# The triangular solves of chunks 2, 4, 6 and 8 handed to the scheduler six operations a step instead of four

## The chip, the cores and the metric

The program runs on one core of a Trainium2 chip. The metric is the device time of one execution in microseconds. The core's engines have instruction queues of their own, which they work off in order: PE (the TensorE, matmuls), DVE (the VectorE), ACT (the ScalarE), POOL (GpSimd) and SP. Here POOL and SP mostly issue DMA transfers.

## The reference

A delta-rule attention over 768 positions (4 batches, 8 heads, 48 features), then two feed-forward blocks on the 3072 resulting rows:

```python
for t in range(S):
    kt, vt, bt = k_n[:, :, t], v[:, :, t], beta[:, :, t, None]
    y[:, :, t] = np.einsum('bhd,bhde->bhe', q[:, :, t], state)
    v_old = np.einsum('bhde,bhd->bhe', state, kt)
    state = state + bt[..., None] * np.einsum('bhd,bhe->bhde', kt, vt - v_old)
# x: y as 3072 rows of 384
h = np.maximum(x @ w_in, 0.0);  x = (h * h) @ w_out          # 384 -> 2048 -> 384
h = np.maximum(np.maximum(x @ w1, x @ w2), x @ w3);  out = h @ w_out2   # 384 -> 768 -> 384
```

## The kernel before

The 768 positions are cut into 12 chunks of 64. Within a chunk the recurrence becomes a triangular system, and its inverse is what the **solve** finds: `solve32` takes two chunks at once (its blocks are 32 x 32), loads the products of keys from DRAM into a tile in `buf`, scales them (`prep`, from ss in L257 to L248), and eliminates column by column (`solve`): 30 steps of one multiply (L278) and one add (L280) on the DVE, then a last multiply (L281). `finish32` stores the result to the DRAM tensor xt (L318, four DMAs on SP's queue). For `HALVED[g]`, that is chunks 2g and 2g + 1, the solve runs in chunk 2g - 2 of the main loop: the solve in chunk 4 is for chunks 6 and 7.

`attention(c)` does the rest of chunk c in ten pieces. `load_x` loads xt into the tile xb (L335, four DMAs on POOL's queue). `st0` multiplies the loaded v by the norms (L421, on the DVE), then does the matmuls pA and pY (L432) and the subtraction r = v - pA (L435, DVE). `zz` makes the transpose xT of xb (L391, DVE) and the matmuls pZ (L398), `ww` the matmuls pW; `mm_u` and `st2` make the outputs and the new state Sb (L467, DVE), and `st3` transposes them and splits them into xh and xl (L507, DVE), the inputs of the feed-forward block. v and kq have two buffers each, and the load of a v (L353, POOL) waits until r has read the one before it in the same buffer.

`moe_a(c)` is the first feed-forward block for chunk c. For each of eight `fp` there is a group `s1` of 18 matmuls into p (L537), then three ACT operations of which the last writes gh (L543), then gl = p - gh on the DVE (L544); two groups later, `s2` makes 18 matmuls of gh and gl into px (L555). p has two buffers, so a group of p waits for the gl of the group before the last. At the chunk's end px is copied to xs and stored (L569, L570).

In the main loop (L773) chunk c runs `moe_a(c)` as the main line with 16 steps, and `steps` (L573) deals the others out beside it: at each step, each of the others has a rate added to its account and is advanced once for every whole number in it. attention(c + 1) has the rate 9/15. A solve in chunk 2, 4, 6 or 8 had the rate 4. Ten advances go by after its loads (`landing=10`), then one for `prep` and one for each step of the elimination. This sets the order in which the operations are written; a scheduler that works with a simulated timeline then sets where each stands in its engine's queue. From chunk 9 on, `load_w3s` loads the weights of the second block (raw, L89, on SP's queue) into a pool of three buffers, which xs shares. After chunk 11 the second block runs (L830, L847).

Of the kernel before, what the change touches and what calls it, by code (L numbers as in the profile page):

```python
# [38 lines left out]
def delta_moe(ctx, tc, kc, ab, kt, vt, beta, beta32, beta16, kq, w_in, w_out, w1, w2, w3, w_out2, out):  # L39
# [157 lines left out]
    def kkps(cs, ps_, dma=nc.sync):  # L197

        todo = [(c, p) for c in cs for p in range(2)]
        ahead = len(kcts) - (len(kcts) < 4)  # L200
        for n in range(min(ahead, len(todo))):
            kkp_load(*todo[n], dma)
        for n, (c, p) in enumerate(todo):
            ks = kss[nk[1] % len(kss)]
            nk[1] += 1
            pk, pq = kk_matmul(c, p, ps_[n % len(ps_)])
            kk_ends[0] = act.copy(ks[:, 0], pk).ins
            kk_ends[1] = vec.tensor_mul(out=ks[:, 1], in0=pq, in1=mask.unsqueeze(1).broadcast_to([128, U2, C])).ins
            for i in mul_after:
                behind(kk_ends[1], i)  # L210
            yield
            kk_store(c, p, ks[:, 0], dma)

            for t in range(2):
                dma.dma_start(p_d[c][64 * t:64 * t + 64, U2 * p:U2 * p + U2], ks[64 - 64 * t:128 - 64 * t, 1])
            if n + ahead < len(todo):
                kkp_load(*todo[n + ahead], dma)
            yield
# [354 lines left out]
    def steps(main, *others):  # L573

        due = [0.0] * len(others)
        for _ in main:
            for i, (rate, g) in enumerate(others):
                due[i] += rate
                while due[i] >= 1.0:
                    due[i] -= 1.0  # L580
                    next(g, None)
        for _, g in others:
            for _ in g:
                pass
# [7 lines left out]
    def w3load(ws):  # L592
        todo = []

        def turned():
            if after:
                after[:], abs_after[:] = last_gl, last_gh
            raw, i, fs = todo.pop(0)
            turn(raw, wh[i][:, :, fs], wl[i][:, :, fs], (KD, 128), vec)

        for i in ws:
            w = (late if i < 2 else wb).tile([128, 2, KD, F2], F32R, name=f"w3_{i}", tag="ABC"[i])
            wh[i], wl[i] = w[:, 0], w[:, 1]
            for f in range(NF2):
                fs = slice(128 * f, 128 * (f + 1))
                todo.append((fetch(w3s[i][:, :, 256 * f:256 * (f + 1)], (KD, 128), nc.sync), i, fs))
                if len(todo) > 1:
                    turned()
                yield
        turned()  # L610

    def load_x2(n, pool_):
        x_h = pool_.tile([128, KD, BT], F32R, name="x_h", tag="x_h")
        x_l = pool_.tile([128, KD, BT], F32R, name="x_l", tag="x_l")
        for j in range(2):
            js = slice(j * TB, (j + 1) * TB)
            xr = conv.tile([128, KD, TB], F32, name="xr", tag="raw", bufs=NR)
            nc.sync.dma_start(xr, x2_d[2 * n + j])
            act.copy(x_h[:, :, js], xr)
            vec.tensor_sub(out=x_l[:, :, js], in0=xr, in1=x_h[:, :, js].bitcast(F32))  # L620
        return x_h, x_l

    def part(g, n):
        for _ in range(n):
            next(g, None)
            yield

    def drain(g):
        for _ in g:
            pass  # L630

    if True:
# [18 lines left out]
        def solve32(g, load=(nc.sync, nc.sync), store=((nc.sync,) * 2,) * 2, landing=0):  # L651
            M, a, ready, norm = start32(g, load)
            for _ in range(landing):
                yield
            if landing:
                prep_after[:] = last_gl
            nm = ready()
            if not landing:
                normed.append(norm(nm))
            yield  # L660
            for n, i in enumerate(solve(vec, M, 32, 64 * len(HALVED[g]), a, tmp32)):
                for j in solve_after:
                    behind(i.ins, j)
                ops.append(i.ins)
                if landing and n == 12:
                    norm(nm)
                yield
            finish32(g, M, store)

        def later(n, g):  # L670
            for _ in range(n):
                yield
            yield from g
# [3 lines left out]
        def weights():  # L677
            for f in range(NF):
                if last_gl[0] and last_gl[0] not in gls:
                    gls.append(last_gl[0])  # L680
                after[:] = gls[-2:-1]
                words(1)
                load_wout(f, vec, nc.sync)
                after.clear()
                prep_after[:] = solve_after[:] = parted[-1:]
                yield
# [86 lines left out]
        for c in range(NC):  # L773
            extra = []
            if c + 1 < NC:
                extra.append((9 / 15.0, attention(c + 1)) if c > 1 else (13 / 15.0, later(3, attention(1))) if not c else (17 / 15.0, later(8, attention(2))))
            if c == 0:
                ws = weights()
                for _ in range(2):
                    next(ws)  # L780
                extra.insert(0, (1.0, ws))
            if c in KK:
                extra.append((1.0, kkps(HALVED[1], (at,), pool)) if c == 0 else (0.8, later(5, kkps(HALVED[2], (at,)))) if c == 1 else (0.6, kkps(HALVED[KK[c]], (at,))))
            if c in SOLVE:
                solve_next = solve32(SOLVE[c], landing=10) if c else solve32(1, (pool,) * 2)
                extra.append((5.0, later(45, part(solve_next, 20))) if c == 0 else (4.0, solve_next))
            if c == 1:
                extra.insert(0, (6.0, solve_next))
            if c == 1:
                kc_after.clear()  # L790
            if c == 1:
                solve_after[:] = last_vec
                prep_after.clear()
            if c == 2:
                solve_after.clear()
            if c == 9:
                after[:] = last_gl
                load_w3s = w3load((0, 1))
            if 9 <= c < NC - 1:
                extra.append((0.4, part(load_w3s, 6)))  # L800
            if c == NC - 1:
                pr.close()
                wb = ctx.enter_context(tc.tile_pool(name="wb", bufs=1, side="right", reuse_waits="tile"))
                drain(load_w3s)
                after.clear()
                abs_after.clear()
                extra.append((0.5, w3load((2,))))
                first = load_x2(0, wb)
            steps(moe_a(c, gp), *extra)
# [112 lines left out]
```

## Time and profile before

| | us |
|---|---|
| median of 3 runs (1000.75 to 1005.13) | 1004.14 |
| the profiled execution | 1003.58 |
| its span, from the first to the last instruction | 1001.9 |
| PE busy | 917.8 |
| DVE busy | 461.1 |
| ACT busy | 407.3 |
| POOL busy | 129.9 |

The first number is what a change is measured by; the sums are made on the profiled execution. Busy time of an engine is time in which at least one of its instructions ran; that of the PE includes waits inside its pipeline. An idle time on the list of an engine's instructions stands in square brackets behind the instruction that ended it, with what that instruction waited for.

### The profile page before, as it was taken

Reading aid. Unit: us, or ns where it says so; the run is one execution under the profiler, and the core shown is the slowest. Engines: PE = TensorE matmul, PEld = TensorE weight load, DVE = VectorE, ACT = ScalarE, POOL = GpSimd, SP = SyncE. Lnnn points to the kernel's source line nnn. Section 1 sums busy time; section 2 is a strip of 40 time slices with the busy share of each in tenths; the row PEclk is TensorE's granted clock in tenths of the full one; section 3 lists DMA queues with packets and bytes.
Section 4 is the critical chain, followed back from the end, with each engine's and each line's share of the span. In section 5 each row is a group of like instructions: output and inputs, shape, how many; then the busy total and the mean of one; then the engine's idle time right before and its main releaser. Section 6 shows DMA issues by size and latency. Waiting matters only on the chain.

```text
span 1001.9 us, 26561 instructions
## 1 busy us (share of the span) xinstructions
PE 917.8 (92%) x11674; PEld 844.7 (84%) x11674; DVE 461.1 (46%) x992; ACT 407.3 (41%) x789; POOL 129.9 (13%) x213
## 2 busy tenths in 40 slices
PE   4067889999999999999999799979999999999998
PEld 4057778999899989999999799979888888888887
DVE  2979796138324832483249144462732323232221
ACT  1947643444444444444453355553521212121111
POOL 2222311121121112112211120000200000000000
PEclk8568988999999999999999899999999999999999
DMA  8938722651463246315621532142400100000001
GB/s 186 329 88 252 226 82 58 163 141 53 133 172 93 60 126 168 97 54 140 152 73 65 122 109 84 49 142 64 152 16 16 47 16 32 17 14 19 9 25 40
DMA packets 74916, 97.25 MB, mean 97 GB/s; under 512 B 35520, under 2 KB 53232, under 8 KB 74800
## 3 DMA queue, kind: packets, MB, share of 16 engines
q1 hardware_dynamic: 54688, 54.22, 19.5%
q0 software_dynamic: 11584, 34.90, 12.3%
q10 hardware_dynamic: 8528, 6.42, 2.2%
q8 instruction: 92, 1.51, 0.6%
q14 instruction: 24, 0.20, 0.1%
HBM read 70.88 MB, written 24.64 MB: 95 GB/s over the span
## 4 chain that ended last, share of the span: by engine, by line
PE 59%; issue 5%; DMA 4%; DVE 3%; POOL 1%; ACT 1%; POOLq 0%; DVEq 0%; ACTq 0%; SPq 0%
PE p L830 23%; PE px L555 12%; PE p L537 12%; PE po L847 8%; DMA xb<-xt 1%; PE pU L442 1%; PE pW L411 1%; PE pY L482 1%; PE pZ L398 1%; DMA v<-in_vt_dram 1%; DVE buf L280 1%; DVE buf L278 1%; DMA xt<-buf 1%; PE pk L190 1%; DVE gl L544 0%
## 5 line engine op out<-in xcount | busy, mean ns | idle before, releaser
L555 PE MATMUL px<-gh,wout 128*128 128x256 f32 x1152 | 219.1, 289 | 4.3 <-ACT gh L543 4.3
L830 PE MATMUL p<-x_h,w 128*128 128x512 f32 x648 | 203.5, 395 | 0.0
L555 PEld LDWEIGHTS px<-gh,wout 128*128 128x128 f32 x1152 | 179.8, 192 | 7.5 <-ACT gh L543 4.7
L537 PE MATMUL p<-xh,win_h 128*128 128x256 f32 x576 | 172.0, 299 | 7.1 <-DVE gl L544 4.9
L537 PE MATMUL p<-xl,win_h 128*128 128x256 f32 x576 | 167.8, 294 | 4.8 <-DVE xl L507 4.8
L537 PE MATMUL p<-xh,win_l 128*128 128x256 f32 x576 | 167.3, 291 | 0.0
L555 PE MATMUL px<-gl,wout 128*128 128x256 f32 x576 | 163.2, 283 | 0.0
L830 PEld LDWEIGHTS p<-x_h,w 128*128 128x128 f32 x648 | 121.6, 188 | 27.2
L544 DVE TENSOR_TENSOR gl<-p,gh 128x512 fp32r<-128x512 f32 x96 | 65.7, 686 | 153.8 <-ACT gh L543 153.8
L830 PE MATMUL p<-x_l,w 128*128 128x512 f32 x324 | 128.1, 395 | 0.0
L537 PEld LDWEIGHTS p<-xh,win_h 128*128 128x128 f32 x576 | 115.1, 200 | 10.8 <-DVE gl L544 6.0
L541 ACT ACTIVATE p<-p 128x512 f32<-128x512 f32 x96 | 55.8, 582 | 158.6 <-PE p L537 157.6
L537 PEld LDWEIGHTS p<-xl,win_h 128*128 128x128 f32 x576 | 114.5, 200 | 6.1 <-DVE xl L507 4.9
L537 PEld LDWEIGHTS p<-xh,win_l 128*128 128x128 f32 x576 | 115.3, 200 | 0.1
L555 PEld LDWEIGHTS px<-gl,wout 128*128 128x128 f32 x576 | 110.7, 192 | 0.0
L836 DVE TENSOR_TENSOR mx<-p,mx 128x512 f32<-128x512 f32 x36 | 24.9, 691 | 128.1 <-PE p L830 127.9
L838 ACT CAST hh<-mx 128x512 fp32r<-128x512 f32 x36 | 22.3, 620 | 126.4 <-DVE mx L837 126.4
L830 PEld LDWEIGHTS p<-x_l,w 128*128 128x128 f32 x324 | 61.0, 188 | 14.5
L278 DVE TENSOR_TENSOR buf<-buf 128x30 f32<-128x30 f32 (+9 forms) x180 | 59.4, 330 | 5.5
L280 DVE TENSOR_TENSOR buf<-buf 128x30 f32<-128x30 f32 (+9 forms) x180 | 59.5, 330 | 5.2
L543 ACT CAST gh<-p 128x512 fp32r<-128x512 f32 x96 | 56.3, 586 | 2.7
L542 ACT ACTIVATE p<-p 128x512 f32<-128x512 f32 x96 | 55.9, 583 | 2.8
(153 smaller groups left out, 1331.9 us busy)
## 6 DMA issues: line engine op xcount, KB each, us to landing
kq<-in_kc_dram POOLq DMA_DIRECT2D x22, 448.0 KB, 4.3
raw<-in_moe_w_dram SPq DMA_DIRECT2D x18, 384.0 KB, 3.3
p<-p POOLq DMA_DIRECT2D x22, 256.0 KB, 3.2
raw<-in_moe_w_out_dram SPq DMA_DIRECT2D x14, 384.0 KB, 3.6
v<-in_vt_dram POOLq DMA_DIRECT2D x24, 192.0 KB, 4.4
ktp<-in_kt_dram POOLq DMA_DIRECT2D x24, 192.0 KB, 3.3
xr<-x SPq DMA_DIRECT2D x12, 384.0 KB, 3.1
out_dram<-os ACTq DMA_DIRECT2D x24, 192.0 KB, 1.9
```

What stands on the lines that cost most here:

```text
L278: eng.tensor_tensor(out=tv, in0=M[:, 0:j, j].unsqueeze(2).broadcast_to([u, j, m]), in1=M[:, j, j + 1:n].unsqueeze(1).broadcast_to([u, j, m ...
L280: yield eng.tensor_tensor(out=M[:, 0:j, j + 1:n], in0=M[:, 0:j, j + 1:n], in1=tv, op=ALU.add)
L537: pe.matmul(p1[:, j], w[:, k, f], x[c][:, k], start=n == 0 and j == 0, stop=n == 8, skip_group_check=True)
L541: act.activation(out=p1, in_=p1, func=AF.Relu)
L542: act.activation(out=p1, in_=p1, func=AF.Square)
L543: last_gh[0] = act.copy(gh, p1).ins
L544: last_gl[0] = vec.tensor_sub(out=gl, in0=p1, in1=gh.bitcast(F32)).ins
L555: pe.matmul(acc[m], w, x[:, j], start=f == 0 and i == 0 and m != 1, stop=f == NF - 1 and i == 2, skip_group_check=True)
L830: pe.matmul(p, w[i][:, k, fs], x[:, k], start=n == 0, stop=n == 8)
L836: vec.tensor_max(out=t, in0=ps[1], in1=t)
L838: act.copy(hh[:, f], t2)
L847: pe.matmul(po[:, 0:DM], x[:, f, js], w[:, f], start=i == 0, stop=i == 17)
```

## The change

One number in L786: the rate of the solves in chunks 2, 4, 6 and 8. The solve of chunk 0, which goes on in chunk 1, has its own rates.

```diff
             if c in SOLVE:
                 solve_next = solve32(SOLVE[c], landing=10) if c else solve32(1, (pool,) * 2)
-                extra.append((5.0, later(45, part(solve_next, 20))) if c == 0 else (4.0, solve_next))
+                extra.append((5.0, later(45, part(solve_next, 20))) if c == 0 else (6.0, solve_next))
```

The same instructions are made; some stand elsewhere in the queues of PE, DVE, ACT and SP. POOL's order is the same.

On the DVE at the start of the solve in chunk 4 (gl is the first block's, ss and r are the solve's; - is before, + is the change):

```order
 L544 TENSOR_TENSOR gl<-p_4227,gh 128x512
 L544 TENSOR_TENSOR gl<-p_4260,gh 128x512
-L544 TENSOR_TENSOR gl<-p_4338,gh 128x512
 L257 COPY ss<-buf 128x32
```

The solve's first operation now stands ahead of one gl more; chunks 2, 6 and 8 have the same piece.

On the DVE at the end of the same solve, where chunk 5 begins (Sb and xl end the attention of chunk 5, xT and r belong to that of chunk 6, v to that of chunk 7, both gl to chunk 5):

```order
 L281 TENSOR_TENSOR buf<-buf,a_4252 128x1024
-L507 TENSOR_TENSOR xl<-pT,xh 128x3x128
-L435 TENSOR_TENSOR r<-v,pA 128x384
-L391 STREAM_TRANSPOSE xT<-xb 128x512
+L467 TENSOR_TENSOR Sb<-pD,Sb 128x384
+L507 TENSOR_TENSOR xl<-pT,xh 128x3x128
+L391 STREAM_TRANSPOSE xT<-xb 128x512
+L435 TENSOR_TENSOR r<-v,pA 128x384
+L421 TENSOR_TENSOR v<-v,normT 128x384
 L544 TENSOR_TENSOR gl<-p_4971,gh 128x512
 L544 TENSOR_TENSOR gl<-p_4996,gh 128x512
-L421 TENSOR_TENSOR v<-v,normT 128x384
```

xT now stands ahead of r, and v, which stood behind the two gl, ahead of them. Chunk 7 begins in the same way. In chunk 3 v stood between the two gl before, and the last gl of chunk 2 now stands behind L281; in chunk 9 v now stands between the first gl and the second.

On the PE at the start of chunk 9 (p_8106 is its second group of p, p_8184 its third, pZ the attention's):

```order
 L537 MATMUL p_8106<-xl,win_h 128x256
-L555 MATMUL px<-gh,wout_791 128x256 x2
-L398 MATMUL pZ<-xb,k_8133 32x32
+L398 MATMUL pZ<-xb,k_8133 32x32 x21
+L555 MATMUL px<-gh,wout_791 128x256 x2
+L398 MATMUL pZ<-xb,k_8133 32x32 x11
 L537 MATMUL p_8184<-xh,win_h 128x256
```

All the pZ now stand ahead of the third group; before, the rest of them stood behind it.

On SP's queue at the same place (xt is the solve's result, raw a load of weights, x the store of xs):

```order
 L318 DMA xt_128<-buf 32x1024 x2
+L89 DMA raw<-in_moe_w_dram 128x3x256 x2
 L570 DMA x_137<-xs 128x512
 L570 DMA x_137<-xs 128x256
-L89 DMA raw<-in_moe_w_dram 128x3x256 x7
+L89 DMA raw<-in_moe_w_dram 128x3x256 x5
```

Two of the loads of weights now stand ahead of the store of xs.

## Rows read from the trace of the kernel before

**Rows 1.** The page, busy us (share of the span) and instructions of two engines.

```profile
PE 917.8 (92%) x11674; PEld 844.7 (84%) x11674; DVE 461.1 (46%) x992; ACT 407.3 (41%) x789; POOL 129.9 (13%) x213
```

**Rows 2.** Timeline of PE: start, us, what, [idle before and its releaser].

```profile
262.92 0.39 PE L537 MATMUL p<-xh,win_h 128*128 128x256 f32 x1 [1.26 <-DVE gl L544]
269.00 0.39 PE L537 MATMUL p<-xh,win_h 128*128 128x256 f32 x1 [0.38 <-DVE gl L544]
362.50 0.38 PE L537 MATMUL p<-xh,win_h 128*128 128x256 f32 x1 [2.16 <-DVE gl L544]
461.23 0.39 PE L537 MATMUL p<-xh,win_h 128*128 128x256 f32 x1 [0.21 <-DVE gl L544]
563.48 0.28 PE L398 MATMUL pZ<-xb,k 32*32 32x32 f32 x2 [5.90 <-DMA xb<-xt]
```

**Rows 3.** Windows: us, busy of each engine, PEclk (granted), DMA share, GB/s.

```profile
core 0: us, PE busy (x) PEld busy (x) DVE busy (x) ACT busy (x) POOL busy (x), PEclk, DMA share, GB/s
360.00:365.00 5.00, 2.84 (x39) 2.70 (x32) 2.63 (x5) 1.55 (x3) 0.29 (x1) 0.86 0.92 260
365.00:370.00 5.00, 5.00 (x90) 4.83 (x89) 1.11 (x2) 2.02 (x4) 0.00 (x0) 0.80 0.33 82
```

**Rows 4.** The chain of waits in order of time: start, us, what.

```profile
357.24 3.82 DMA xb<-xt
...
457.51 2.35 DMA xb<-xt
...
555.69 7.02 DMA xb<-xt
...
571.44 2.34 PE p L537 x18
```

**Rows 5.** Timeline of DVE, end of the solves in chunks 2 and 4.

```profile
253.58 1.22 DVE L281 TENSOR_TENSOR buf<-buf,a 128x1024 f32<-128x1024 f32 x1
...
334.22 0.69 DVE L544 TENSOR_TENSOR gl<-p,gh 128x512 fp32r<-128x512 f32 x1 [0.75 <-ACT gh L543]
...
338.22 0.41 DVE L280 TENSOR_TENSOR buf<-buf 128x240 f32<-128x240 f32 x1
338.66 0.41 DVE L278 TENSOR_TENSOR buf<-buf 128x240 f32<-128x240 f32 x1
...
351.03 0.55 DVE L467 TENSOR_TENSOR Sb<-pD,Sb 128x384 f32<-128x384 f32 x1
...
352.77 1.23 DVE L281 TENSOR_TENSOR buf<-buf,a 128x1024 f32<-128x1024 f32 x1
...
355.18 0.55 DVE L435 TENSOR_TENSOR r<-v,pA 128x384 f32<-128x384 f32 x1 [0.53 <-PE pA L432]
361.16 0.71 DVE L391 STREAM_TRANSPOSE xT<-xb 128x512 f32<-128x512 f32 x1 [5.42 <-DMA xb<-xt]
```

**Rows 6.** Timelines of POOL, DVE and SP: loads issued, and v waiting for its load.

```profile
258.58 2.61 POOL L335 DMA_DIRECT2D xb<-xt  x4 [7.63 <-DMA xt<-buf]
261.18 0.55 POOL L351 DMA_DIRECT2D kq<-in_kc_dram  x1
261.72 0.58 POOL L353 DMA_DIRECT2D v<-in_vt_dram  x1
...
267.79 0.56 DVE L421 TENSOR_TENSOR v<-v,normT 128x384 f32<-128x384 f32 x1 [4.93 <-DMA v<-in_vt_dram]
...
356.57 2.62 POOL L335 DMA_DIRECT2D xb<-xt  x4 [6.93 <-DMA xt<-buf]
...
392.29 0.54 POOL L351 DMA_DIRECT2D kq<-in_kc_dram  x1 [5.47 <-PE pY L432]
394.19 0.55 POOL L353 DMA_DIRECT2D v<-in_vt_dram  x1 [1.36 <-DVE r L435]
397.20 0.56 DVE L421 TENSOR_TENSOR v<-v,normT 128x384 f32<-128x384 f32 x1 [2.84 <-DMA v<-in_vt_dram]
...
555.12 2.65 SPq L89 DMA_DIRECT2D raw<-in_moe_w_dram  x3
```

## The prediction, made before the changed kernel was run

> **What bounds the kernel now.** I read the page's busy times first: the TensorE (PE) is busy for 92% of the span, the VectorE (DVE) for 46% [rows 1]. So a change on the DVE pays only where the PE stands still for it. The PE's own list of instructions comes next, for the idle time ahead of each [rows 2]. It stands still at the four places where a chunk with a solve has ended and the next has begun: 1.26 us at the start of chunk 3 (and 0.38 us at 269.00), 2.16 us in chunk 5, 0.21 us in chunk 7 and 5.90 us in chunk 9. I call these places A, B, C and D. After B and D the PE also runs slowly: the granted clock is 0.86 and 0.80 in the two stretches after B's stall [rows 3], so it had fallen to the 1.2 GHz level and come back to 2.4. At B that costs 5 x 0.14 + 5 x 0.20 = 1.7 us.
>
> The chain of waits and the DVE's own list tell what happens there. The solve's last multiply (L281) starts at 352.77 [rows 5]; its result is stored to DRAM, loaded again as xb, and the transpose xT, which stands in the DVE's queue ahead of the next chunk's gl, starts at 361.16 after 5.42 us of idling [rows 5]. Eight microseconds pass between solve and transpose. The PE waits for that gl because p has two buffers and gl frees one. At D the load alone takes 7.02 us, at B 3.82, at C 2.35 [rows 4]: three w3 loads (raw) are issued beside it at D [rows 6].
>
> **The change, part by part.** Nothing is added or removed; the solve is only handed over earlier. In the order on the DVE, ss (the solve's first operation) moves ahead of one gl, so the solve begins that much earlier. How much of it reaches the end is set on the way: the gl among its steps are still held by the PE. The one at 334.22 waited 0.75 us for its gh [rows 5], and cannot move. From there I count. Before, 19 of the solve's steps follow it; in the changed order 15.5. A step is two operations that start 0.44 us apart [rows 5], so 3.5 x 0.88 = 3.1 us, less some 0.3 us as v (L421) now waits a little longer. An Sb of 0.5 us (351.03, [rows 5]) now stands behind L281. The sum is 3.3 us at B, C and D; at A the chunk's last gl (0.6 us) goes behind L281 too, and one half step more is done, so 4.5 us. The gl that A delays ends about 0.5 us before the PE needs it: cover enough, and lost only if the solve slips.
>
> But the transposition is not the last thing in front of gl any more. Before, r (L435) ran at 355.18 while the DVE waited for xb [rows 5]. Now xT stands ahead of r, and v (L421) between r and gl (A, B, C) or between the first two gl (D). v needs a load that POOL issues behind the four xb loads and kq, and that load overwrites a buffer that r reads. So the new chain is xb, xT, r, load of v, v, gl. The load of v is the unknown. It took 3.0 us where it was issued 1.9 us after kq (394.19 to 397.20), and 6.1 us where it was issued 0.54 us after it (261.72 to 267.79) [rows 6]. In the new order it goes out some 2.5 us after kq, which is like the first row; beside it run the same stores as in the second. I take 3.6 us and keep 3.0 and 6.1 for the range.
>
> Place B: L281 starts at 349.5. From there to xT it was 8.4 us before (352.77 to 361.16), or 6.9 us with C's load in place of B's (1.5 us shorter, [rows 4]). I take xT at 357.2. r ends 1.1 us later, at 358.3, the load of v lands at 361.9, v and the wait for its end take 0.5 us, gl ends 0.7 us after that, and the PE goes on at 363.1. Before, it went on at 362.50 [rows 2]: +0.6 us, so the earlier solve is used up by the new wait.
>
> At A, B and C the PE runs dry at 261.66, 360.34 and 461.02 (each start in [rows 2] less its idle time), so the same course stands 98.7 us earlier at A and 100.7 us later at C. At C the PE goes on at 463.8, where it had gone on at 461.23 [rows 2]: +2.6 us. A stall of 2.8 us is longer than B's 2.16, which ended in the low clock, so C pays 1.7 us for the clock as well.
>
> At A the solve ends 1.2 us earlier still, but its store took 1.2 us longer than B's: from L281 to the first load of xb 5.0 us (253.58 to 258.58) against 3.8 (352.77 to 356.57) [rows 5, 6]. So the PE goes on at about 264.2, against 262.92: +1.3 us. The 0.38 us at 269.00 go, since v no longer holds a gl there: +0.9 us.
>
> Place D gains. With L281 3.3 us earlier, xb lands between 556.2 (B's 3.82 us) and 559.4 (its own 7.02 us); before it landed at 562.71 [rows 4]. I take 557.0, just when the PE runs out of work (563.48 less 5.90, [rows 2]). The pZ matmuls, which the new order draws together ahead of the matmuls of p, start at once, the first gl ends at 558.9, and the PE does 18 matmuls of p and 16 of px at the full clock. The second gl is behind v: r ends at 558.1, the load takes 4.5 us here, v and gl end at 563.9. There the next group of p starts, which started at 571.44 before [rows 4]: -7.5 us, which contains the clock.
>
> **Sum:** 0.9 + 0.6 + (2.6 + 1.7) - 7.5 = -1.7 us on the profiled run of 1003.6 us (its span 1001.9 us and 1.7 us around it), which stands 0.6 us under the median of the three runs, 1004.14. The forecast is 1001.9 us.
>
> **Rivals.** (1) The load of v lands late, slower. If it takes 6.1 us, as in the second row, all four places move by 2.5 us: -1.7 + 10 = +8.3, or 1011.9 us. It decides from 5.3 us on, since 4 x 1.7 us takes the sum past +5 us. For it speaks that the same kq and stores are about; against it, that kq has a lead of 2.5 us instead of 0.54. (2) The load of v is quick, faster. With 3.0 us and an xT one microsecond earlier, A comes to -0.7, B to -1.0, C to +1.0 without a fall of the clock, and D to -8.5: -9.2 us, or 994.4 us. The 3.0 us row speaks for it. (3) D gains little. On SP's queue two of the w3 loads now stand ahead of the store of xs, directly behind the solve's stores, so they start earlier as well and run beside the xb loads again. If those take 7.02 us once more, xb lands at 559.4, the PE stands for 2 us, the clock falls (1.7 us), v is as late as the loads were, and D is left with about -2: +3.8 us, or 1007.4. Against it: two loads instead of three, with a start ahead of xb. (4) The earlier handing over is taken back by the DVE, which is full in the solve, and nothing moves: 1003.6 us. Against it speaks the order, in which 3.5 steps have changed sides of a gl that the PE fixes.
>
> On rival 3 the Trainium skill says, in "DMA: Bandwidth & Descriptors", section "Queues, rings and completion order", that each DMA engine takes turns between the queues that have work for it, packet by packet. By that rule the w3 loads on SP's queue would hold up the xb loads on POOL's wherever they meet, and the sum would be rival 3's. The 7.02 us at D against 2.35 at C agree with it; they do not show how much two loads that start earlier will take.
>
> **How the numbers follow.** Main course 0.50 (between about 998.5 and 1006 us), rival 1 0.16, rival 2 0.22, rival 3 0.08, rival 4 0.04. A measurement of this kernel can tell about 0.5%, 5 us, from no change. Faster by more: rival 2 and the lower edge of the main course, 0.28. Slower by more: rival 1 and some of rival 3, 0.20. Within: 0.52. The range reaches to the ends of rivals 1 and 2, cut by two microseconds at the upper end: 994.5 to 1010. The main course alone spans 998.5 to 1006.
>
> **What would show it.** In the changed profile L281 should start some 3.3 us earlier at B, C and D against the chunk's gl, xT should wait for xb less than 5.4 us, and v should be idle for the DMA of v right before gl at A, B and C. The PE's list should show a stall of 2 to 3 us at A, B and C each, and next to none at D. The forecast is wrong if v waits nowhere (then rival 2), if v's load takes over 5 us, if D's stall is still there, or if a new stall stands inside the solve, where gl now shares the DVE with steps that come earlier.

## The result: 0.9% slower, and the profile after

The changed kernel took 1012.44 us (median of 4 runs, 1011.01 to 1014.85), the kernel before 1003.66 us beside it (median of 4, 1000.75 to 1005.13). The ratio is 1.0091, with a 95% interval of 1.0064 to 1.0119. The forecast was 1001.9 us in a range of 994.5 to 1010. The profiled execution took 1013.34 us with a span of 1010.1 us, 8.2 us more than before.

To see where they lie I cut both spans at the same instruction, the second gh of the chunk in which a solve runs. These are its starts on the ACT, before and after (columns as in [rows 5]):

```profile
214.44 0.58 ACT L543 CAST gh<-p 128x512 fp32r<-128x512 f32 x1
313.79 0.58 ACT L543 CAST gh<-p 128x512 fp32r<-128x512 f32 x1
414.47 0.58 ACT L543 CAST gh<-p 128x512 fp32r<-128x512 f32 x1
511.64 0.58 ACT L543 CAST gh<-p 128x512 fp32r<-128x512 f32 x1
```

```profile
213.32 0.59 ACT L543 CAST gh<-p 128x512 fp32r<-128x512 f32 x1
318.40 0.59 ACT L543 CAST gh<-p 128x512 fp32r<-128x512 f32 x1
419.54 0.59 ACT L543 CAST gh<-p 128x512 fp32r<-128x512 f32 x1
522.54 0.59 ACT L543 CAST gh<-p 128x512 fp32r<-128x512 f32 x1
```

Each stretch holds one place: A between the first two marks, D between the last mark and the end of the span. The kernels of the experiments below are cut in the same way:

| kernel, us of its profiled span | to the mark | with A | with B | with C | with D | span |
|---|---|---|---|---|---|---|
| before | 214.4 | 99.4 | 100.7 | 97.2 | 490.3 | 1001.9 |
| changed | 213.3 | 105.1 | 101.1 | 103.0 | 487.6 | 1010.1 |
| v behind gl | 213.3 | 100.5 | 97.0 | 97.0 | 487.9 | 995.6 |
| r ahead of xT | 213.2 | 101.0 | 101.4 | 98.4 | 488.3 | 1002.3 |
| stores of xs behind xb | 215.6 | 106.5 | 97.2 | 97.0 | 488.0 | 1004.3 |
| v behind gl, raw behind xb | 213.7 | 97.6 | 97.0 | 97.0 | 481.2 | 986.4 |
| rate 6 in chunk 8 alone | 214.3 | 99.4 | 100.3 | 97.2 | 488.1 | 999.3 |
| rate 4, raw behind xb | 214.7 | 100.2 | 99.3 | 97.2 | 488.3 | 999.7 |
| v behind gl, raw behind xb, r ahead of xT | 212.3 | 97.6 | 97.0 | 97.0 | 483.1 | 986.9 |
| the same, stores of xs behind xb | 215.8 | 97.6 | 97.0 | 97.0 | 480.9 | 988.2 |

Each row is one execution. Three of the kernels (before, rate 6 in chunk 8 alone, and rate 4 with raw behind xb) have the same order at A to C, and still differ by 0.8 us at A, 1.4 at B and 0.1 at C; a difference of that size between two rows tells nothing. The row of the stores of xs behind xb is its slowest execution of ten, 1005.98 us against a median of 999.36.

The change costs 5.7 us at A, 0.5 at B (within that spread) and 5.8 at C, and gains 2.7 at D. The 1.1 us ahead of A stay unexplained; there the ten kernels differ by up to 3.5 us. A stretch in which the PE never waits lasts 97.0 us. The PE's own list of the changed kernel has the stalls, where [rows 2] had those of before:

```profile
266.31 0.58 PE L537 MATMUL p<-xh,win_h 128*128 128x256 f32 x1 [5.77 <-DVE gl L544]
367.65 0.38 PE L537 MATMUL p<-xh,win_h 128*128 128x256 f32 x1 [2.63 <-DVE gl L544]
469.92 0.58 PE L537 MATMUL p<-xh,win_h 128*128 128x256 f32 x1 [3.76 <-DVE gl L544]
570.57 0.28 PE L398 MATMUL pZ<-xb,k 32*32 32x32 f32 x2 [2.51 <-DMA xb<-xt]
571.37 1.28 PE L398 MATMUL pZ<-xb,k 32*32 32x32 f32 x40 [0.52 <-DMA xb<-xt]
```

At A the stall has grown from 1.26 to 5.77 us, at C from 0.21 to 3.76. At D it has shrunk from 5.90 to 2.51 + 0.52 us. Windows of the changed kernel around A and C (columns as in [rows 3], PEclk is the third number from the end):

```profile
260.00:265.00 5.00, 0.54 (x38) 0.40 (x28) 0.36 (x1) 1.72 (x4) 0.58 (x1) 0.83 0.65 184
265.00:270.00 5.00, 3.69 (x17) 3.69 (x18) 2.35 (x4) 0.00 (x0) 0.00 (x0) 0.50 0.23 51
...
465.00:470.00 5.00, 1.24 (x66) 1.10 (x65) 1.30 (x3) 2.24 (x5) 0.51 (x1) 0.81 0.64 172
470.00:475.00 5.00, 5.00 (x24) 5.00 (x25) 1.06 (x2) 0.81 (x2) 0.00 (x0) 0.50 0.31 73
```

Behind both stalls the granted clock is 0.50, the level of 1.2 GHz; before the change it was 1.00 in all four of these windows. What that costs stands in the chain of waits. Its part at C, in order of time (start, us, what), reads like this:

```profile
464.93 3.68 DMA v<-in_vt_dram
...
469.18 0.69 DVE gl L544
...
469.92 4.21 PE p L537 x18
474.12 2.58 PE px L555 x18
```

The chain goes through the load of v and gl into the PE. Eighteen matmuls of p take 4.21 us there and the 18 of px 2.58 us. The same two groups at C in the kernel before, at the full clock:

```profile
461.23 2.42 PE p L537 x18
463.64 2.16 PE px L555 x18
```

So the clock costs 1.79 + 0.42 = 2.2 us at C, and at A, where the chain has 4.11 us for the matmuls of p, 1.7. The stalls grew by 5.77 - 1.26 - 0.38 = 4.1 us at A and by 3.55 at C. The two sums, 5.8 and 5.8 us, answer to the 5.7 and 5.8 us of the table.

The DVE's list at A shows what gl stood behind (its counterpart is in [rows 5] and [rows 6]):

```profile
259.21 0.71 DVE L391 STREAM_TRANSPOSE xT<-xb 128x512 f32<-128x512 f32 x1 [4.36 <-DMA xb<-xt]
259.84 0.52 DVE L435 TENSOR_TENSOR r<-v,pA 128x384 f32<-128x384 f32 x1
265.09 0.56 DVE L421 TENSOR_TENSOR v<-v,normT 128x384 f32<-128x384 f32 x1 [4.73 <-DMA v<-in_vt_dram]
265.57 1.28 DVE L544 TENSOR_TENSOR gl<-p,gh 128x512 fp32r<-128x512 f32 x2
```

And POOL's list shows why v was late: its load waits 3.91 us for r, which stands behind xT, which waits for xb.

```profile
253.59 2.61 POOL L335 DMA_DIRECT2D xb<-xt  x4 [3.75 <-DMA xt<-buf]
256.20 0.55 POOL L351 DMA_DIRECT2D kq<-in_kc_dram  x1
260.66 0.58 POOL L353 DMA_DIRECT2D v<-in_vt_dram  x1 [3.91 <-DVE r L435]
```

At D the same chain of waits reads as follows; [rows 4] had 7.02 us for the load of xb there.

```profile
564.29 6.94 DMA xb<-xt
...
571.37 1.28 PE pZ L398 x40
...
574.14 3.79 PE p L537 x18
577.93 1.91 PE px L555 x16
579.84 2.16 PE p L537 x18
```

Two theories were left to tell apart. **Chain**: the PE is held because gl stands behind v in the DVE's queue, and v's load behind r and xT. **Loads**: the loads of xb land late because the store of xs (A, B, C) or the loads of raw (D) run beside them. The second was the prediction's rival 3 for D; at A to C the prediction had not considered it.

### The profile page after: what moved, and what is told of

It reads as the page before. It is cut to its first block, busy times and chain, and to the rows that moved or that the text cites. A ratio compares the mean times of both kernels' runs of the same rounds, so it can differ in the third digit from the quotient of the medians.

```text
span 1010.1 us, 26557 instructions
## 1 busy us (share of the span) xinstructions
PE 922.9 (91%) x11674; PEld 849.5 (84%) x11674; DVE 460.7 (46%) x992; ACT 407.7 (40%) x789; POOL 130.0 (13%) x213
## 4 chain that ended last, share of the span: by engine, by line
PE 69%; issue 10%; DVE 9%; DMA 7%; ACT 2%; POOL 2%; ACTq 0%; POOLq 0%; DVEq 0%; SPq 0%
PE p L830 22%; PE p L537 15%; PE px L555 14%; PE po L847 7%; DMA v<-in_vt_dram 2%; DVE buf L280 2%; DVE buf L278 2%; PE pU L442 2%; PE pZ L398 1%; PE pY L482 1%; PE pW L411 1%; DMA xb<-xt 1%; DMA xt<-buf 1%; DMA buf<-kk 1%; PE pk L190 1%
```

## The experiments

**v behind gl.** One thing undone in the changed kernel: v (L421) stands behind the second gl at all four places. On the DVE four rows move, on the other engines none.

```diff
-            if c < 2:
-                behind(i.ins, last_gl[0] if c else solved[0])
+            if c < 2 or c in (5, 7, 9, 11) and not p:
+                behind(i.ins, gl_of[c - 2, 1] if c > 1 else last_gl[0] if c else solved[0])
...
-            gs[fp] = (gh, gl)
+            gs[fp], gl_of[c, fp] = (gh, gl), last_gl[0]
```

> The changed kernel (1012.4 us) with one thing undone: at A, B, C and D the multiply v (L421) stands behind the second gl of the new chunk again; only four rows on the DVE differ. Theory 'chain': the PE is held at A, B and C because gl stands behind v, whose load can only be issued after r, which itself stands behind xT. With v out of the way gl starts when xT and r are done: at A some 260.5 instead of 265.7, so the stall falls from 5.77 us to about 1 us, at B and C (2.63 and 3.76 us) it disappears, and with the stalls go the falls of the granted clock at A and C (about 1.8 and 2.3 us). Sum: 6.6 + 2.6 + 6, at D 0 to 2: 15 to 17 us, so 995 to 998 us. Theory 'loads': the xb loads land late because stores and loads of weights run beside them, and v only waits in time that is lost to that anyway; then xT is as late as in the changed kernel and no more than 5 us come back: 1007 to 1012 us.

Measured: 995.98 us, 0.9945 (0.9917 to 0.9974) of the kernel before. The chain theory's number is met. The PE's only stall at A, B and C is this one, and the DVE's list shows gl directly behind r, with v waiting where nobody waits for it:

```profile
263.39 0.39 PE L537 MATMUL p<-xh,win_h 128*128 128x256 f32 x1 [0.79 <-DVE gl L544]
```

```profile
261.58 0.71 DVE L391 STREAM_TRANSPOSE xT<-xb 128x512 f32<-128x512 f32 x1 [4.66 <-DMA xb<-xt]
262.21 0.52 DVE L435 TENSOR_TENSOR r<-v,pA 128x384 f32<-128x384 f32 x1
262.65 1.43 DVE L544 TENSOR_TENSOR gl<-p,gh 128x512 fp32r<-128x512 f32 x2
267.21 0.56 DVE L421 TENSOR_TENSOR v<-v,normT 128x384 f32<-128x384 f32 x1 [3.12 <-DMA v<-in_vt_dram]
```

B and C come to 97.0 us, 4.1 and 6.0 less than in the changed kernel. A comes to 100.5; 2.0 us of that are a wait at the start of the solve in chunk 2. The solve's first operation, ss, waits 3.22 us there for its load (it starts at 217.86). In the changed kernel it waited 0.62 us, and before, where it came at 219.74, not at all, so the earlier solve has lost its cover over this load as well. D is unchanged (487.9 against 487.6): v ahead of the second gl costs nothing there.

**r ahead of xT.** The other thing undone, v left ahead of gl:

```diff
-            if c == 1:
-                behind(last_vec[0], last_gl[0])
+            if c == 1 or c in (4, 6, 8, 10):
+                behind(last_vec[0], last_gl[0] if c == 1 else r_of[c, 0])
...
-            vec.tensor_sub(out=r, in0=v, in1=pA)
+            r_of[c, p] = vec.tensor_sub(out=r, in0=v, in1=pA).ins
```

> The changed kernel with the other thing undone: at A, B, C and D the subtraction r (L435) stands ahead of the transpose xT again, as before the change; v stays ahead of gl. Only four pairs of rows on the DVE differ. Theory 'chain': r runs while the DVE waits for xb, so the load of v is issued 2 to 5 us earlier and lands about when xT is done; at A v would run at some 263 instead of 265.7, at B and C 1 to 3 us earlier, and the falls of the clock at A and C may go: 6 to 13 us less, 999 to 1007 us, which is between the changed kernel and the one with v behind gl. Theory 'loads': the load of v now runs beside the xb loads and takes them longer, nothing is gained: 1010 to 1014 us.

Measured: 1003.64 us, 1.0032 (1.0002 to 1.0062), in the middle of the chain theory's range. The load of v goes out early, beside the loads of xb and kq, and now takes longer: at B it is issued at 357.06 and v runs at 362.51, 5.45 us later, where the changed kernel took 2.79 (363.64 to 366.43). DVE of this kernel, v at A and then the three at B:

```profile
261.15 0.56 DVE L421 TENSOR_TENSOR v<-v,normT 128x384 f32<-128x384 f32 x1 [2.51 <-DMA v<-in_vt_dram]
...
355.68 0.56 DVE L435 TENSOR_TENSOR r<-v,pA 128x384 f32<-128x384 f32 x1 [0.53 <-PE pA L432]
357.77 0.71 DVE L391 STREAM_TRANSPOSE xT<-xb 128x512 f32<-128x512 f32 x1 [1.53 <-DMA xb<-xt]
362.51 0.56 DVE L421 TENSOR_TENSOR v<-v,normT 128x384 f32<-128x384 f32 x1 [4.03 <-DMA v<-in_vt_dram]
```

So at B the PE waits 2.88 us, no less than in the changed kernel. At A and C the early issue does help: against the mark v runs 3.8 and 2.4 us earlier there, and the stalls are 1.96 and 1.37 us instead of 5.77 and 3.76. But with v ahead of gl the PE still waits at all three places.

**Stores of xs behind xb.** The stores of xs of chunks 2, 4 and 6 are written into the next chunk and issued from POOL behind the loads of xb:

```diff
-            nc.sync.dma_start(x2_d[c][:, 2 * i:2 * i + n], xs[:, 2 * i:2 * i + n])
+            late_xs.append((x2_d[c][:, 2 * i:2 * i + n], xs[:, 2 * i:2 * i + n])) if c in (2, 4, 6) else nc.sync.dma_start(x2_d[c][:, 2 * i:2 * i + n], xs[:, 2 * i:2 * i + n])
...
+            s1(fp), [behind(pool.dma_start(*x).ins, xb_of[c + 1]) for x in late_xs if fp == 3], fp == 3 and late_xs.clear()
```

> The changed kernel, with the stores of xs of chunks 2, 4 and 6 taken off SP's queue and issued from POOL, behind the four xb loads; order on the DVE as in the changed kernel at A, B and C. It measures the loads by themselves. Theory 'loads': at A the xb loads took 5.6 us from the first issue to xT (2.99 before the change, when the store of xs was 1.3 us ahead of them), at B 4.05 and at C 4.30; without the store they take about 3 us, xT, r, the load of v and gl all come 2.6, 1.0 and 1.3 us earlier, in all 4 to 7 us with the clock: 1005 to 1008 us. Theory 'chain' alone: xb takes what it takes, 4 to 5.6 us, and the stalls at A, B and C stay within 1 us: 1010 to 1014 us.

Measured: 999.36 us, 0.9979 (0.9957 to 1.0001), less than either theory gave, and the reason is that the expectation was wrong about the order: at B and C the scheduler also put v between the two gl. So only A tells of the stores alone. There xT comes 4.48 us after the first issue of xb (258.92 to 263.40) instead of 5.62, the load of v takes 3.06 us instead of 4.43, and the PE's stall falls from 5.77 to 2.68 us. A's stretch is long all the same (106.5 us): the beginning of the solve in chunk 2 takes 3.6 us more than in the changed kernel, and ss waits 3.28 us for its load there. At B and C both stalls are gone, and both stretches come to 97 us; with one gl ahead of it, v does no harm.

**v behind gl, raw behind xb.** The first kernel, and the first two loads of w3 issued from POOL behind the loads of xb:

```diff
-        raws.append(dma.dma_start(raw.rearrange(f"p {names} t -> p {flat}"), src).ins)
+        raws.append(dma.dma_start(raw.rearrange(f"p {names} t -> p {flat}"), src).ins), dma is pool and 10 in xb_of and behind(raws[-1], xb_of[10])
...
-                todo.append((fetch(w3s[i][:, :, 256 * f:256 * (f + 1)], (KD, 128), nc.sync), i, fs))
+                todo.append((fetch(w3s[i][:, :, 256 * f:256 * (f + 1)], (KD, 128), pool if i == 0 and f < 2 else nc.sync), i, fs))
```

> The kernel with v behind the second gl, and at D the first two loads of w3 (raw) issued from POOL behind the four xb loads instead of from SP's queue beside them; nothing else differs from it. Theory 'loads at D': the xb loads took 7.9 us from the first issue to xT at D, and 4.05 to 5.6 us at A, B and C, where no w3 loads run; without these beside them xb lands 2.3 to 3.9 us earlier, the stalls of 2.51 and 0.52 us ahead of pZ go, and the fall of the clock with them (granted 0.55 in 570 to 575 us, some 2 us): 3 to 6 us less than the kernel with v behind gl. If the w3 loads don't matter to xb: within 1 us of it.

Measured: 989.94 us (median of 4, of which one took 997.01), 0.9896 (0.9849 to 0.9942), and 6.0 us less than the first kernel in the same comparison. The first kernel's chain at D and the two kernels' issues there show it. First kernel, chain of waits and SP's list:

```profile
548.56 7.41 DMA xb<-xt
...
558.93 4.14 PE p L537 x18
```

```profile
546.20 0.99 SPq L89 DMA_DIRECT2D raw<-in_moe_w_dram  x2
547.46 0.84 SPq L570 DMA_DIRECT2D x<-xs  x2
```

This kernel, POOL's and the DVE's list, and a window with the PE busy throughout and the clock at 1.00:

```profile
545.12 2.61 POOL L335 DMA_DIRECT2D xb<-xt  x4 [3.99 <-DMA xt<-buf]
547.73 1.53 POOL L89 DMA_DIRECT2D raw<-in_moe_w_dram  x2
```

```profile
549.72 0.71 DVE L391 STREAM_TRANSPOSE xT<-xb 128x512 f32<-128x512 f32 x1 [3.57 <-DMA xb<-xt]
```

```profile
550.00:555.00 5.00, 5.00 (x94) 4.65 (x93) 2.16 (x4) 3.64 (x8) 0.60 (x1) 1.00 0.96 316
```

From the first issue of xb to xT it is 4.60 us (545.12 to 549.72), against 8.62 in the first kernel (547.25 to 555.87). The loads theory holds at D: 4.0 us of the load, and with the stall the fall of the clock. The edit moves the two loads of raw to another queue and also starts them later; which of the two it takes is not shown.

**Rate 6 in chunk 8 alone**, to have D by itself:

```diff
-                extra.append((5.0, later(45, part(solve_next, 20))) if c == 0 else (6.0, solve_next))
+                extra.append((5.0, later(45, part(solve_next, 20))) if c == 0 else (6.0 if c == 8 else 4.0, solve_next))
```

> The rate 6 for the solve in chunk 8 alone; the solves in chunks 2, 4 and 6 have the rate 4 again, so A, B and C are those of the kernel before and D is that of the changed kernel. By the account of the two traces D is worth 490.3 - 487.6 = 2.7 us: 999.5 us, with L281 three us earlier, an xb load of 7 to 8 us from its first issue to xT, and 2 to 3 us of stall ahead of pZ. If the prediction's step for D was right and the loss of the changed kernel at C had hidden it: 7.5 us, 994.7 us.

Measured: 1000.24 us, 0.9975 (0.9956 to 0.9995), 2.1 us less than the kernel before beside it (1002.35). The account's 2.7 us is right, the prediction's 7.5 is not. From the first issue of xb to xT it is 7.93 us here.

**Rate 4, raw behind xb.** The kernel before, with the same edit of the loads as above.

> The kernel before, rate 4, with the first two loads of w3 (raw) issued from POOL behind the four xb loads at D instead of from SP's queue beside them. Theory 'loads at D': xb takes 4.6 to 5.6 us from its first issue to xT instead of 7.8, the stall of 5.90 us falls to about 3, and 3 to 4 us are gained: 998 to 999.5 us, which leaves 8 to 10 us to the kernel with the rate 6, v behind gl and the same two loads moved (989.9 us); so the earlier solve is worth that much once nothing waits behind v. If the earlier solve is worth nothing by itself and the moved loads did it all: 990 to 992 us.

Measured: 1001.22 us, 0.9991 (0.9977 to 1.0005). Neither theory's number: the gain is 1.1 us, not 3 to 4. PE at D:

```profile
561.28 0.28 PE L398 MATMUL pZ<-xb,k 32*32 32x32 f32 x2 [4.47 <-DMA xb<-xt]
```

xT, which reads what two of the four loads bring, came 3.76 us after the first issue, but pZ needs the other two, the last among them, and started only 5.72 us after it (555.56 to 561.28; before, 555.03 to 563.48 is 8.45). And that first issue came 5.7 us after the start of L281 here, 4.9 before. So the stall fell by 1.4 us alone. The other half of the expectation holds: the median is 11.3 us behind that of the kernel with rate 6 (989.94 us), and by the ratios to the kernel before beside each (0.9991 and 0.9896) it is 9.5 us; 8 to 10 were expected.

**v behind gl, raw behind xb, r ahead of xT**: the fourth kernel with the second one's edit.

> Rate 6, v behind the second gl, the two w3 loads behind the xb loads (the kernel that took 989.9 us), and r ahead of xT again at A to D. Theory 'chain': at A the first gl starts up to 0.6 us earlier and A's stretch of 97.62 us comes down to the 96.96 us of B and C; at B, C and D the PE doesn't wait and nothing moves: 989.3 us, within 1 us of it. If the load of v, now issued beside the xb loads, holds these up as the stores do: A to D get up to 1 us longer each, 990 to 994 us.

Measured: 989.25 us, 0.9869 (0.9848 to 0.9889). That is 12.0 us faster than the kernel with rate 4 and raw behind xb beside it, and not to be told apart from the 989.94 us of the fourth kernel. The expected time is met; that A would come down to 97.0 us is not. A's stretch holds 0.6 us more than B's and C's already in chunk 2, and the PE has no stall there to lose.

**The same, stores of xs behind xb:**

> The kernel before this one in the list, and the stores of xs of chunks 2, 4 and 6 issued from POOL behind the xb loads. It measures what the store of xs costs the xb loads, with the order on the DVE held: from first issue to xT 5.0 to 6.2 us at A and 3.7 to 4.3 us at B and C with the store beside them, 4.5 and 3.1 us where it stood behind them. Theory 'loads': 1 us shorter at each of A, B, C. No stall of the PE is left there, so the time is the same within 1 us: 989 us.

Measured: 990.0 us, 0.9872 (0.9848 to 0.9897), the same. It gives the price of the store. From the first issue of xb to xT, in us:

| | A | B | C | D |
|---|---|---|---|---|
| before | 2.99 | 4.59 | 3.04 | 7.78 |
| changed | 5.62 | 4.05 | 4.30 | 7.89 |
| all three edits | 5.40 | 3.84 | 3.72 | 5.06 |
| the same, stores of xs behind xb | 4.47 | 2.96 | 2.99 | 4.73 |

A store of xs beside the loads costs them 0.7 to 0.9 us, at each of A, B and C; these are single executions, and at A the three kernels with the order of before differ by up to 0.6 us in the same figure. At A they take 1.5 us longer than at B and C with or without it; why stays open.

## Why the prediction was wrong

**Right: the earlier solve.** At B L281 started 352.77 - 313.79 = 38.98 us after the mark ([rows 5]), and now 354.35 - 318.40 = 35.95: 3.0 us earlier. In the same way it is 3.1 us at C and D and 4.3 at A; 3.3 and 4.5 were forecast. Rival 4 is out.

**Right: the new chain.** xb, xT, r, load of v, v, gl holds the PE at A, B and C, as described. Undoing one link of it gave back all that was lost at B and C, and at A all but the 2.0 us at the start of the solve.

**Right in size: the load of v.** It took 4.4, 2.8, 3.8 and 3.7 us at A to D, 3.7 on average, where 3.6 was taken at A to C, and 4.5, for which no row was given, at D. Rival 1 gave nearly the measured time (1011.9 us), but not by its mechanism.

**B was right** (+0.6 forecast, +0.5 measured), in part by luck: in the time of before, which is 4.6 us earlier there, xT came at 357.6 instead of 357.2, 0.3 us passed between the end of r and the issue of the load, which the forecast had left out, and the load was 0.8 us shorter than taken.

**Wrong: A (+0.9 forecast, +5.7 measured).** Three terms. First the loads of xb. The forecast's xT at A is B's 357.2 less 98.7, or 258.5; measured it is 259.21, and 260.3 in the time of before (the mark lies 1.1 us earlier): 1.8 us. The step took the loads' time from the trace of before. But with the solve earlier the store of xs and the loads of xb, which had gone out 1.3 us apart (257.32 and 258.58), go out together (253.63 and 253.59). By the last table 0.9 us are the store's; the rest stays open. Second the load of v with 4.4 us, not 3.6, and issued 0.3 us after r ends: 1.1 us. Third the clock: by the prediction's own numbers the PE was to stand for 2.5 us at A (261.66 to 264.2), longer than B's 2.16 us behind which the clock had fallen; it counted the clock at C for that reason and forgot it at A. That is 1.7 us. Together it is 4.6 of the 4.8 us.

**C was undersized (+4.3 forecast, +5.8 measured)**: the stall 3.76 instead of 2.8 us, and the clock 2.2 instead of 1.7. The 1.7 us had been read at B, where the chain of before gives 1.5 (18 matmuls of p in 3.36 us and of px in 2.69, against 2.42 and 2.16): the forecast's windows counted time in which the PE stood still.

**Wrong: D (-7.5 forecast, -2.7 measured).** The step that failed is the landing of xb, which was taken near the lower of two bounds (557.0, between 556.2 and 559.4). Against the mark, which lies 10.9 us later, xT at 570.22 is 559.3, the upper bound; and the last of the four loads, which pZ needs, landed at 571.23 by the chain, or 560.3, past it. The mechanism was rival 3's, with a chance of 0.08. Two loads of raw instead of three, started 1.2 us ahead of xb instead of beside it, cost it as much as the three had (7.89 us from the first issue to xT, before 7.78). The Trainium skill's rule that each DMA engine takes turns between its queues packet by packet ("DMA: Bandwidth & Descriptors", "Queues, rings and completion order") pointed this way. The runs agree with its sign: the same loads on xb's own queue, behind it and started later, took 4.0 us off. No run here shows the turns themselves.

Of the 4.8 us between forecast and result 3.3 are the landing (560.3 instead of 557.0). The rest is the clock, which the forecast had full here: the matmuls of p behind pZ take 3.79 us. In the kernel with v behind gl and raw behind xb, where the PE did not stand, the chain has 2.35 us for them:

```profile
552.47 2.35 PE p L537 x18
```

v, whose wait the forecast put last at D, ran at 575.32, well ahead of the group at 579.84 that needed its gl.

**The sum** for A, B and C was +5.8 and came to +12.0. In spans, 1000.2 us was forecast and 1010.1 measured: these 6.2 us and D's 4.8, less the 1.1 ahead of A, are the 9.9 between them.

**What the prediction didn't see** is that the earlier solve is worth some 10 to 12 us (1001.22 against 989.25 us; of the 12.8 us between the two profiled spans 10.4 lie at A to D) once two things are out of its way that have nothing to do with it: v, which is wanted a chunk later, ahead of gl in a queue, and raw, which nobody waits for, beside xb on the DMA engines.

## What to carry to other kernels

A change in a scheduler's rates is judged by what it puts into the queues of the waiting engines: look for an operation that is wanted late, waits for a load, and now stands ahead of one that is wanted at once, and pin it behind. When a step comes earlier, so do its transfers, and they meet others than before: a load's duration from the old trace is not its duration there (from 2.99 to 5.62 us at A, from 4.59 to 4.05 at B). Where the forecast has a stall as long as one behind which the clock fell, the cost of the clock belongs in the sum or in a rival at every such place, not only at the one where one thinks of it.

## What was unexpected in the hardware

How long the PE stood did not decide by itself whether the granted clock fell. With r ahead of xT it stood 1.96 us at A, up to 262.36, and the clock was 0.73 in that window; with rate 4 and raw behind xb it stood 2.55 us at A, up to 264.42, and 2.34 us at B, and the clock stayed at 1.00. In both kernels the last matmuls ahead of the stall at A are those of pk and pq (L190). The windows at A, of the first and then of the second:

```profile
260.00:265.00 5.00, 3.04 (x40) 2.90 (x33) 2.35 (x4) 1.61 (x3) 0.00 (x0) 0.73 0.61 169
265.00:270.00 5.00, 5.00 (x94) 4.83 (x93) 0.69 (x1) 2.19 (x4) 0.00 (x0) 0.93 0.17 38
```

```profile
260.00:265.00 5.00, 2.45 (x76) 2.18 (x75) 1.29 (x2) 2.91 (x6) 3.30 (x6) 1.00 0.78 220
265.00:270.00 5.00, 5.00 (x98) 4.87 (x96) 1.26 (x3) 1.75 (x3) 0.00 (x0) 1.00 0.70 188
```

And the four loads of xb, 64 KB each, took anything from 2.9 to 8.6 us from the first issue to the transpose that reads them, the longest where loads of raw ran beside them on another queue.
